# The last 156 words of a hand-written order, rearranged: an attention and dense layer on one core

## The chip, the cores and the metric

The kernel runs on one core of a Trainium2 chip. The metric is the device time of one execution in microseconds (us), the median of several runs. The core's engines have queues of their own and run each queue in order: TensorE (PE, with its weight loads shown as PEld), VectorE (DVE), ScalarE (ACT), GpSimd (POOL) and SyncE (SP), which here issues nearly all DMAs.

## The reference, cut to what matters

```python
xn = layernorm(x)                                   # x: [1, 2048, 512], bf16
# A: attention in 4 segments of 512 tokens, 32 heads of 16, with a memory M, z
q, k, v = xn @ wq, xn @ wk, xn @ wv
for s in range(4):
    p = softmax(qs @ ks.T * scale + causal_mask);  a_dot = p @ vs
    a_mem = (phi(qs) @ M) / (phi(qs) @ z + 1e-6)    # memory of the segments before
    o = g * a_mem + (1 - g) * a_dot                 # g = sigmoid(beta), by head
    M += phi(ks).T @ vs;  z += phi(ks).sum()
A = o @ wo
B = silu(xn @ w1) @ w2                              # dense layer, 1792 wide
return x + A + B
```

## The kernel before, in words

The 2048 tokens are four segments of four 128-token tiles. Channels lie in four groups `dt` of 128 (eight heads each), the dense layer's 1792 features in 14 tiles. Outputs of A and B are summed in one PSUM accumulation: an output tile of 128 tokens by 512 columns takes 18 products, 14 with the dense layer's `hT` and `w2`, 4 with the attention's `oT` and `wo`. They may come in any order.

Nothing is scheduled automatically. One long string, `ORDER` (lines 16 to 98), is a list of words, and a loop (line 795) emits the piece of work that each word names. The order of the words is therefore the order in every engine's queue. The words at the end of the list are:

- `S76` and so on: scores of a batch (line 653): PE's products, then ACT's exponential of 128x2048 and POOL's causal mask. All scores share one tile of four PSUM banks, `psS`.
- `E15`, `O15`: products of the weights with V for the even and odd heads (line 687). `Ev15`, `Oa15` copy the sums out (DVE, ACT), and SP moves rows of them by small DMAs (`zraw`, `oraw`).
- `h3.11.0`, `ha`, `hv`: the dense layer's first product (two halves), its tanh on ACT (line 457), its multiply on DVE (line 462).
- `R0.2`, `W0`, `R1.*`, `W1`: reciprocals and weights of the softmax sums (DVE, lines 525 and 531).
- `z3.1`, `d3.1`: SP spreads the weights over partitions by two DMAs each into an `spr` buffer (line 542; four buffers). `zv`, `dv` multiply with them (lines 554 and 564), `n3.1` is the memory's product on PE, `nv` adds it into `oT` (line 573).
- `o3.0.12`: product 12 of output tile 0 of segment 3, all 512 columns. `oc` is a half of the columns, `od` a quarter. `oh12.1` is product 12 of the last tile, right half; the last tile is made as two halves of 256 columns.
- `xl3.0`: SP loads 128 rows of x for the residual into `x_res` (line 579). `st3.0`: DVE evicts the output tile, adding the residual (line 586), and SP stores it (line 591). `sh0`, `sh1`: the same for the halves of the last tile (lines 633 and 637).

Output tiles 0 and 1 of the last segment lie in banks of a pool of four (`pp`), which the dense layer, the sums and the memory's products also use. Tile 2 and the two halves of tile 3 lie in a last allocation of the four-bank tile of the scores, called `fin`, one bank each:

```python
                if "fin" not in st:
                    st["fin"] = psatt.tile([P, 4, L], F32, name="psS")
                st["psO", *key] = st["fin"][:, half or j, 0:width]
```

The kernel takes away the wait of a product for the eviction of another output in `fin` (lines 617 to 621); the wait of an eviction for the products is left to the framework. A pool hands out its buffers in the order in which they came free in the list. After a word of scores the products are whole (128x128 weights, line 322); after `E` or `O` they are issued as four products of 32 weight columns each (line 324).

Of the kernel before, what the change touches and what calls it, by code (L numbers as in the profile page):

```python
# [91 lines left out]
S73 h3.2.1 ha3.2 Ev14 oc2.2.5.1 o2.1.2 o2.2.16 o2.1.6 hv3.12 h3.8.0 o2.2.10 st2.2 hv3.2 o2.1.1 o2.1.5 h3.8.1 ha3.8 hv3.8  # L92
S79 o2.1.0 O14 Ov14 od2.1.12.2 s3 sv3 r3.1 o2.1.7 r3.3 h3.7.0 r3.2 r3.0 oc2.1.10.0 od2.1.12.3 o2.1.3 w3
S77 h3.6.0 R0.0 oc2.1.11.0 h3.7.1 R0.1 ha3.7 h3.6.1 hv3.7 d3.2 o2.1.14 R0.3 h3.9.0 ha3.6 hv3.6 o2.1.15
S76 o2.1.8 d3.0 d3.1 h3.9.1 o2.1.9 oc2.1.10.1 h3.13.0 ha3.9 od2.1.12.0 oc2.1.11.1 h3.13.1 xl3.3 hv3.9 o3.0.12 od2.1.12.1 o2.1.4 o3.0.1 o2.1.13 ha3.13
S75 dv3.2 R0.2 W0 o3.0.7 hv3.13 o3.0.4 h3.10.0 z3.2 o2.1.16 h3.10.1 z3.1 o3.0.2 o3.0.8 dv3.0 o3.0.9 o3.0.0 z3.0 ha3.10 hv3.10
S78 o3.0.5 h3.11.0 o2.1.17 st2.1 h3.11.1 E15 o3.0.6 o3.2.1 oh1.1 o3.1.8 Ev15 ha3.11 oc3.0.3.1 oh0.1 O15 oh12.1 o3.2.3 o3.2.5 hv3.11 zv3.1 oh5.1 o3.2.8 n3.2 Oa15 oh13.0 o3.1.3 o3.1.12 dv3.1 zv3.2 nv3.2 o3.2.7 oc3.0.11.1 oc3.0.11.0 oh9.0 n3.0 oh16.0 n3.1 zv3.0 o3.2.9 o3.1.1 oc3.1.0.1 o3.1.13 o3.2.0 oc3.1.0.0 o3.2.12 o3.2.6 nv3.0 od3.1.11.2 nv3.1 oh11.1 o3.1.14 oh15.1 o3.2.11 oh0.0 R1.1 R1.0 oh10.0 o3.0.14 od3.0.10.2 oh8.0 od3.1.11.3 d3.3 oh15.0 od3.0.10.0 R1.3 o3.1.6 R1.2 oc3.1.9.0 oc3.1.9.1 o3.1.5 oh2.0 o3.1.10 W1 oh14.0 o3.2.13 oh1.0 o3.1.15 oh5.0 o3.0.15 o3.0.16 dv3.3 z3.3 od3.0.10.1 o3.2.15 xl3.1 o3.2.16 zv3.3 o3.2.2 n3.3 oh11.0 od3.1.11.1 oh3.1 oh10.1 oh6.0 oh4.1 nv3.3 o3.1.4 od3.0.10.3 oh4.0 oh12.0 o3.2.4 o3.0.13 oc3.0.3.0 oh3.0 o3.0.17 xl3.0 st3.0 o3.2.14 od3.1.11.0 oh7.0 o3.2.17 oh17.0 oh7.1 sh0 o3.2.10 o3.1.2 oh2.1 o3.1.7 o3.1.16 st3.2 o3.1.17 oh17.1 st3.1 oh6.1 oh13.1 oh14.1 oh16.1 oh8.1 oh9.1 sh1
"""


# [733 lines left out]
```

## Time and profile before

| | |
|---|---|
| median of 3 runs | 228.55 us (228.1 to 229.02) |
| the profiled execution | 229.09 us |
| its span, first to last instruction | 227.4 us |
| granted TensorE clock | 1.00 |
| PE busy | 217.2 us (96%) |
| DVE, ACT, POOL busy | 177.7, 198.0, 113.9 us |
| first product of S76, the first word on the changed lines | 200.01 us |
| last product begins | 223.32 us |
| last DVE eviction, `sh1` | 223.88 us, 0.41 long |
| last store issued | 224.77 us |

The span is what the profile shows; the run's time also has what lies around it, 1.7 us here. The page gives the busy time of each engine; the chain of waits follows the work that ended last back from the end; the timeline lists instructions in order of time. An instruction's line in it ends with the idle time before it and what ended that.

### The profile page before, as it was taken

What the parts mean: (1) busy time and instruction counts of PE and PEld (TensorE: products, weight loads), DVE (VectorE), ACT (ScalarE), POOL (GpSimd) and SP (SyncE); (2) the same over time, 40 slices, a digit from 0 to 9 for tenths busy, and PEclk for the clock granted to TensorE, in tenths of its full rate; (3) what the DMA queues carried; (4) which work ended last, traced back from release to release, by engine and by line L of the source; (5) the groups of instructions that cost most, each with busy time, mean ns of one, the idle gap of its engine ahead of it and who ended that gap; (6) DMA issues with size and microseconds to landing.
All of it is one profiled execution on the core that took longest, in us unless ns stands there. A gap on an engine that the chain in (4) does not pass through costs nothing.

```text
span 227.4 us, 7543 instructions
## 1 busy us (share of the span) xinstructions
PE 217.2 (96%) x3124; PEld 112.9 (50%) x3152; DVE 177.7 (78%) x351; ACT 198.0 (87%) x179; POOL 113.9 (50%) x173
## 2 busy tenths in 40 slices
PE   8999999999999999999999999999999999999993
PEld 8666645545534434444444434445444444445662
DVE  5799899987787897658798798747676888887834
ACT  3799998999999999999999899999999989897000
POOL 6059647667454673665644577546474265342000
PEclk9999999999999999999999999999999999999999
DMA  6992429323215213404314212141032212024122
GB/s 181 361 381 68 77 52 299 60 55 57 61 22 158 72 35 47 96 15 112 41 40 113 75 53 58 35 117 42 22 100 66 88 36 84 29 63 130 29 90 94
DMA packets 34787, 20.55 MB, mean 90 GB/s; under 512 B 15680, under 2 KB 34240, under 8 KB 34752
## 3 DMA queue, kind: packets, MB, share of 16 engines
q1 hardware_dynamic: 32128, 17.45, 28.3%
q10 hardware_dynamic: 2624, 2.62, 3.6%
q8 instruction: 24, 0.39, 0.8%
q14 instruction: 11, 0.09, 0.1%
HBM read 9.96 MB, written 2.10 MB: 53 GB/s over the span
## 4 chain that ended last, share of the span: by engine, by line
PE 62%; ACT 11%; DVE 11%; DMA 8%; issue 4%; SPq 2%; POOL 0%; DVEq 0%
PE ps L322 18%; PE psO L322 14%; PE psS L662 9%; ACT Pb L669 8%; PE ps L324 8%; PE psO L324 6%; PE psV L696 6%; DMA x_hi<-in_A_x_dram 4%; DMA spr<-rz 3%; ACT th L457 2%; DMA x_res<-in_A_x_dram 2%; DVE stats L272 1%; DVE o_out L586 1%; DVE kT L361 1%; PE psM L324 1%
## 5 line engine op out<-in xcount | busy, mean ns | idle before, releaser
L669 ACT ACTIVATE Pb<-psS 128x2048 bf16<-128x2048 f32 x80 | 150.2, 1878 | 5.8 <-PE psS L662 5.1
L677 POOL TENSOR_SCALAR_AFFINE_SELECT Pb<-Pb 128x512 bf16<-128x512 bf16 (+1 forms) x112 | 80.1, 729 | 85.1 <-ACT Pb L669 83.7
L462 DVE SCALAR_TENSOR_TENSOR hT<-th,ps 128x512 bf16<-128x512 bf16 x56 | 37.8, 679 | 14.1 <-ACT th L457 13.7
L322 PE MATMUL ps<-xnT,w_sb 128*128 128x512 bf16 (+1 forms) x177 | 43.3, 340 | 0.8 <-issue 0.5
L322 PE MATMUL psO<-w_sb,hT 128*128 128x512 bf16 (+2 forms) x139 | 36.1, 340 | 0.7 <-issue 0.5
L457 ACT ACTIVATE th<-ps 128x512 bf16<-128x512 f32 x56 | 32.8, 597 | 0.5 <-PE ps L322 0.4
L324 PE MATMUL psO<-w_sb,hT 128*32 128x128 bf16 (+2 forms) x468 | 26.7, 300 | 0.0
L322 PEld LDWEIGHTS <-w_sb 128*128 128x128 bf16 x184 | 17.1, 98 | 16.3 <-issue 3.3
L696 PE MATMUL psV<-Pb,Vz 128*32 128x128 bf16 (+3 forms) x512 | 23.1, 300 | 0.4 <-DVE oT L573 0.2
L322 PEld LDWEIGHTS <-hT 128*128 128x128 bf16 x149 | 13.6, 97 | 16.9 <-issue 4.8
L324 PE MATMUL ps<-xnT,w_sb 128*32 128x512 bf16 (+1 forms) x384 | 21.8, 329 | 0.0
L324 PEld LDWEIGHTS <-hT 128*32 128x32 bf16 x636 | 15.7, 97 | 9.7 <-issue 1.7
L696 PEld LDWEIGHTS <-Vz 128*32 128x32 bf16 x512 | 13.0, 96 | 10.6 <-issue 1.4
L662 PE MATMUL psS<-qT,kT 16*128 16x128 bf16 (+3 forms) x256 | 17.3, 301 | 0.9 <-ACT Pb L669 0.8
L662 PE MATMUL psS<-qT,kTo 32*128 32x384 bf16 (+3 forms) x256 | 17.2, 299 | 0.6 <-ACT Pb L669 0.2
L362 POOL TENSOR_SCALAR kTo<-kT,pm_odd 128x512 bf16<-128x512 bf16 x16 | 11.9, 747 | 8.2 <-DVE kT L361 7.3
L322 PE MATMUL ps<-xnT,wk_sb 128*128 128x512 bf16 (+1 forms) x66 | 15.4, 328 | 0.7 <-issue 0.5
L322 PE MATMUL ps<-wv_sb,xnT 128*128 128x512 bf16 x48 | 14.3, 380 | 0.6 <-issue 0.2
L662 PEld LDWEIGHTS <-kT 16*128 16x128 bf16 x256 | 5.9, 91 | 16.7 <-issue 16.2
L361 DVE CAST kT<-ps 128x512 bf16<-128x512 f32 x15 | 10.2, 687 | 4.6 <-PE ps L322 4.3
L586 DVE SCALAR_TENSOR_TENSOR o_out<-psO,x_res 128x512 bf16<-128x512 f32 x14 | 9.6, 687 | 5.3 <-PE psO L322 2.8
L719 DVE CAST oraw<-psV 128x512 bf16<-128x512 f32 x16 | 11.0, 688 | 3.4 <-PE psV L696 3.3
(105 smaller groups left out, 298.3 us busy)
## 6 DMA issues: line engine op xcount, KB each, us to landing
spr<-rz SPq DMA_DIRECT2D x56, 64.0 KB
x_res<-in_A_x_dram SPq DMA_DIRECT2D x16, 128.0 KB
out_dram<-o_out SPq DMA_DIRECT2D x15, 128.0 KB
w_sb<-in_B_w_dram SPq DMA_DIRECT2D x1, 1792.0 KB
w_sb<-in_B_w_dram ACTq DMA_DIRECT2D x1, 1792.0 KB
x_hi<-in_A_x_dram SPq DMA_DIRECT2D x2, 512.0 KB
oraw<-odd SPq DMA_DIRECT2D x64, 16.0 KB
wv_sb<-in_A_wv_dram SPq DMA_DIRECT2D x2, 256.0 KB
```

The costliest lines, as they stand in the source:

```text
L322: return [nc.tensor.matmul(out, lhsT=lhsT, rhs=rhs, start=start, stop=stop, skip_group_check=True)]
L324: nc.tensor.matmul(out[c : c + 32], lhsT=lhsT[:, c : c + 32], rhs=rhs, start=start, stop=stop, tile_position=(0, c), skip_group_check=True,)
L361: copy(out=kT[:, dt, :], in_=sts[s].pop(("k", dt))[:, :])
L362: nc.gpsimd.tensor_scalar(out=kTo[:, dt, :], in0=kT[:, dt, :], scalar1=pm_odd[:, 0:1], scalar2=1.0, op0=ALU.mult, op1=ALU.mult,)
L457: nc.scalar.activation(out=th[:], in_=sts[s]["h", ft][:, :], func=AF.Tanh, scale=0.5)
L462: nc.vector.scalar_tensor_tensor(out=st["hT"][:, ft, :], in0=st.pop(("th", ft))[:], scalar=1.0, in1=st.pop(("h", ft))[:, :], op0=ALU.add, ...
L586: out = nc.vector.scalar_tensor_tensor(out=o_out[:], in0=st.pop(("psO", j)), scalar=0.5, in1=st["x", j][:], op0=ALU.mult, op1=ALU.add)
L662: nc.tensor.matmul(psS[:, g, c0 : c0 + nq], lhsT=kk[rows, dt, kt * P : (kt + 1) * P], rhs=st["qT"][rows, dt, kt * P : L], start=True, stop ...
L669: exp = nc.scalar.activation(out=Pb[:, :, :], in_=psS[:, :, :], func=AF.Exp, scale=SCALE)
L677: mask = nc.gpsimd.affine_select(out=blocks, in_=blocks, compare_op=ALU.is_ge, fill=0.0, base=0, pattern=[[0, blocks.shape[1]], [1, P]], c ...
L696: nc.tensor.matmul(psV[32 * g : 32 * g + 32, kt * P : L], lhsT=Vzs[s % 2][:, kt, 4 * dt + g, par : par + 2, :].rearrange("p a d -> p (a d) ...
L719: copy(out=oraw[:], in_=sts[s].pop(("psV", 0))[:, :])
```

## The change

Four lines of `ORDER` are replaced by three with the same 171 words. The first 15 words keep their places. In the new order the scores S78 and the dense products `h3.11` come earlier, the eviction `st2.1` of segment 2's last open tile comes much later, the `z` moves go 0, 1, 2 in place of 2, 1, 0, `dv3.2` comes after `dv3.0`, and the five stores come in the order `sh1`, `sh0`, `st3.0`, `st3.2`, `st3.1` with up to four words of products between them; in the old order `st3.0`, `sh0`, `st3.2`, `st3.1`, `sh1`, with up to seven.

```diff
-S76 o2.1.8 d3.0 d3.1 h3.9.1 o2.1.9 oc2.1.10.1 h3.13.0 ha3.9 od2.1.12.0 oc2.1.11.1 h3.13.1 xl3.3 hv3.9 o3.0.12 od2.1.12.1 o2.1.4 o3.0.1 o2.1.13 ha3.13
-S75 dv3.2 R0.2 W0 o3.0.7 hv3.13 o3.0.4 h3.10.0 z3.2 o2.1.16 h3.10.1 z3.1 o3.0.2 o3.0.8 dv3.0 o3.0.9 o3.0.0 z3.0 ha3.10 hv3.10
-S78 o3.0.5 h3.11.0 o2.1.17 st2.1 h3.11.1 E15 o3.0.6 o3.2.1 oh1.1 o3.1.8 Ev15 ha3.11 oc3.0.3.1 oh0.1 O15 oh12.1 o3.2.3 o3.2.5 hv3.11 zv3.1 oh5.1 o3.2.8 n3.2 Oa15 oh13.0 o3.1.3 o3.1.12 dv3.1 zv3.2 nv3.2 o3.2.7 oc3.0.11.1 oc3.0.11.0 oh9.0 n3.0 oh16.0 n3.1 zv3.0 o3.2.9 o3.1.1 oc3.1.0.1 o3.1.13 o3.2.0 oc3.1.0.0 o3.2.12 o3.2.6 nv3.0 od3.1.11.2 nv3.1 oh11.1 o3.1.14 oh15.1 o3.2.11 oh0.0 R1.1 R1.0 oh10.0 o3.0.14 od3.0.10.2 oh8.0 od3.1.11.3 d3.3 oh15.0 od3.0.10.0 R1.3 o3.1.6 R1.2 oc3.1.9.0 oc3.1.9.1 o3.1.5 oh2.0 o3.1.10 W1 oh14.0 o3.2.13 oh1.0 o3.1.15 oh5.0 o3.0.15 o3.0.16 dv3.3 z3.3 od3.0.10.1 o3.2.15 xl3.1 o3.2.16 zv3.3 o3.2.2 n3.3 oh11.0 od3.1.11.1 oh3.1 oh10.1 oh6.0 oh4.1 nv3.3 o3.1.4 od3.0.10.3 oh4.0 oh12.0 o3.2.4 o3.0.13 oc3.0.3.0 oh3.0 o3.0.17 xl3.0 st3.0 o3.2.14 od3.1.11.0 oh7.0 o3.2.17 oh17.0 oh7.1 sh0 o3.2.10 o3.1.2 oh2.1 o3.1.7 o3.1.16 st3.2 o3.1.17 oh17.1 st3.1 oh6.1 oh13.1 oh14.1 oh16.1 oh8.1 oh9.1 sh1
+S76 o2.1.8 d3.0 d3.1 h3.9.1 o2.1.9 oc2.1.10.1 h3.13.0 ha3.9 od2.1.12.0 oc2.1.11.1 h3.13.1 xl3.3 hv3.9 o3.0.12 ha3.13 o3.0.8 R0.2 o2.1.17 o3.0.6 o3.0.2 o2.1.4
+S75 o3.0.9 h3.11.0 hv3.13 h3.10.0 o2.1.16 h3.10.1 o2.1.13 o3.0.0 oc3.0.3.0 ha3.10
+S78 od2.1.12.1 W0 h3.11.1 z3.0 dv3.0 o3.0.1 hv3.10 E15 o3.0.4 ha3.11 od3.0.10.1 dv3.2 oc3.0.3.1 z3.1 z3.2 Ev15 o3.0.13 o3.0.5 oh4.0 o3.2.12 oh0.0 oh2.1 hv3.11 zv3.0 oh5.1 od3.0.10.0 O15 dv3.1 oh3.1 oh7.1 n3.0 zv3.1 oh6.1 o3.2.13 Oa15 oh6.0 oh12.0 od3.0.10.3 o3.1.13 d3.3 o3.1.1 nv3.0 o3.1.8 oh3.0 n3.2 od3.0.10.2 o3.2.10 oh0.1 o3.1.3 zv3.2 o3.2.8 oh8.0 nv3.2 R1.1 oh13.1 oh10.1 od3.1.11.1 o3.0.7 oh16.0 R1.2 oh16.1 oh14.0 oc3.1.9.1 R1.3 R1.0 oh14.1 oh13.0 oh2.0 o3.1.16 o3.1.12 oh9.0 o3.2.0 o3.1.10 o3.2.7 oh1.1 n3.1 oh5.0 o3.1.2 oh10.0 o3.1.6 o3.1.4 W1 o3.2.9 oh12.1 nv3.1 oc3.1.0.1 z3.3 xl3.1 oh7.0 od3.1.11.0 o3.0.14 o3.2.14 oh8.1 oc3.0.11.0 st2.1 dv3.3 zv3.3 o3.0.16 o3.2.4 o3.2.11 o3.2.2 oh11.0 oh15.0 oh9.1 n3.3 oh15.1 xl3.0 o3.1.5 oh11.1 oh4.1 nv3.3 o3.2.15 oh1.0 o3.0.15 oh17.1 od3.1.11.2 o3.2.16 oh17.0 oc3.0.11.1 o3.2.1 o3.2.3 o3.0.17 o3.2.5 o3.2.17 sh1 o3.2.6 o3.1.15 oc3.1.9.0 od3.1.11.3 sh0 o3.1.7 st3.0 o3.1.17 o3.1.14 st3.2 oc3.1.0.0 st3.1
```

## The prediction

> **What bounds the kernel now.** I read, in this order, the page's busy times, the busy time by stretch over the last 27 us, the chain that ended last, and the timeline of the end. The first 15 words of the changed list are the old ones, so nothing before 202.5 us of the span (start of `o3.0.8`) can move.
>
> ```profile
> PE 217.2 (96%) x3124; PEld 112.9 (50%) x3152; DVE 177.7 (78%) x351; ACT 198.0 (87%) x179; POOL 113.9 (50%) x173
> ```
>
> ```profile
> 205.00:210.00 5.00, 5.00 (x98) 2.56 (x100) 3.58 (x7) 3.54 (x4) 1.27 (x2) 1.00 0.39 120
> 210.00:215.00 5.00, 5.00 (x128) 3.12 (x120) 4.21 (x10) 0.59 (x1) 0.00 (x0) 1.00 0.16 43
> 215.00:220.00 5.00, 5.00 (x148) 3.45 (x144) 2.52 (x7) 0.00 (x0) 0.00 (x0) 1.00 0.37 111
> 220.00:223.60 3.60, 3.60 (x96) 2.30 (x88) 2.08 (x5) 0.00 (x0) 0.00 (x0) 1.00 0.09 28
> 223.60:227.40 3.80, 0.00 (x1) 0.00 (x0) 0.69 (x2) 0.00 (x0) 0.00 (x0) 1.00 0.36 116
> ```
>
> Columns: the stretch, its length, busy us of PE, PEld, DVE, ACT, POOL, then the granted clock. PE is full to 223.60 at clock 1.00. Laying its products end to end from S76 (200.01), at 0.216 us for 512 columns (0.43 for two: 216.27, 216.38 and 216.59 in the timeline), I find no wait for data, only about 0.2 us at each change between score tiles and the rest. So 223.60 is a floor that the same products in another order can't undercut. What is left is the 3.78 us behind it.
>
> ```profile
> 208.37 3.75 DMA spr<-rz
> ...
> 212.21 0.44 DVE oT L554
> ...
> 216.91 0.60 SPq L542
> 217.51 0.04 issue
> 217.56 0.46 SPq L579
> 218.01 0.04 issue
> 218.06 3.60 DMA x_res<-in_A_x_dram
> ```
>
> ```profile
> 221.75 0.69 DVE L586 SCALAR_TENSOR_TENSOR o_out<-psO,x_res 128x512 bf16<-128x512 f32 x1 [1.52 <-PE psS L324]
> ...
> 222.35 0.41 DVE L633 SCALAR_TENSOR_TENSOR o_half<-psS,x_res 128x256 bf16<-128x256 f32 x1
> ...
> 222.69 0.68 DVE L586 SCALAR_TENSOR_TENSOR o_out<-psS,x_res 128x512 bf16<-128x512 f32 x1
> ...
> 223.21 0.39 PE L324 MATMUL psS<-w_sb,hT 128*32 128x256 bf16 x8
> 223.28 0.68 DVE L586 SCALAR_TENSOR_TENSOR o_out<-psO,x_res 128x512 bf16<-128x512 f32 x1
> 223.41 0.92 SPq L591 DMA_DIRECT2D out_dram<-o_out  x2
> 223.88 0.41 DVE L633 SCALAR_TENSOR_TENSOR o_half<-psS,x_res 128x256 bf16<-128x256 f32 x1
> 224.77 0.34 SPq L637 DMA_DIRECT2D out_dram<-o_half  x1
> ```
>
> The five evictions stand on DVE without a gap: 0.60 us from a full one to the next, 0.34 after a half. The first waited for its x_res, whose load took 3.60 us; but the last, `sh1`, could not have begun before PE's end plus 0.05 (the row of `st2.1`: product done 207.55, eviction 207.60), that is 223.65, and began 223.88. So the late load costs 0.23 at the end, not the 1.5 us that the chain suggests. From the last issue at 224.77 the store lands at 226.53 by the landing records (1.76; full stores took 1.73 to 1.80), and the closing of the program takes 0.85 to 227.38.
>
> **The change, part by part.**
>
> *Products.* Same words, so the same 479 products from S76 on. Whole and 32-column forms both take 0.216 us for 512 columns, so the seven words that change form with S78's earlier place cost 0, and the changes of form stay as many. No term.
>
> *The scores move.* Between `o3.0.12` and S75 there are now five full products (1.08 us) for three and a quarter (0.70): S75 comes 0.38 later, at 203.74. From S75 to S78 there is 2.27 of products for 2.38: S78 comes at 206.45 for 206.18. ACT was idle before both exponentials (0.46 and 0.44 us, waiting for PE), so they shift with the scores, S78's to 206.89 to 208.77, and POOL's mask to 208.90 to 209.54. Queued behind: `oh4.0`, first user of the four banks that this exponential reads, arrives at 208.84 with the banks ready at 208.82; `O15` arrives at 206.45 + 0.33 + 2.75 = 209.54, and started 0.05 after the mask before (209.27, 209.32). It can start at 209.59: **+0.05 us**. If that cover goes, each further tenth of lateness is a tenth. Bounds 0 to 0.15.
>
> *DVE.* `R0.2` comes before `hv3.13`, `dv3.2` only after `hv3.10`. Walking DVE with its row durations: `hv3.13` ends 204.64 and `h3.10.0`, which takes its bank, arrives at 204.73; `hv3.10` ends 207.28, `E15` arrives at 207.48; `nv3.0` ends 211.6, `n3.2` arrives at 211.9. All hidden by PE's own work, with 0.04 to 0.3 us to spare.
>
> *SP's queue.* It loses `st2.1` ahead of the moves of `zraw` (0.45 us), which goes between the two last x_res loads instead; the three `z` moves are reordered. `z3.0` takes the free buffer, `z3.1` that of `dv3.0` (free at 205.25), `z3.2` that of `dv3.2` (free at 207.62), so `z3.2` is issued at 207.68 and 208.33 in place of `z3.0`'s 207.73 and 208.37: SP loses nothing. That slot is the one whose landing took 3.75 us; half-moves otherwise land about 2.1 after issue. If the slot is late again, `z3.2` lands at 212.1, `nv3.2` ends at 213.37, and `oh16.0`, which reads it, arrives at 213.55: hidden by 0.13. Behind it `R1.*` waits for `zraw` (213.1), `W1` ends by 215.5 (before: 216.24), and `d3.3` then `z3.3` go out at 214.7 to 216.75 (before to 216.91). `z3.3` lands at 218.8; `n3.3` arrives on PE at 219.13 and ends 219.51, `nv3.3` 219.55 to 220.25, and `oh17.1`, first reader of the last quarter of oT, arrives at 220.43. Hidden by 0.13. I put **0** for these, bounds 0 and 0.3.
>
> *The x_res loads.* `xl3.0` leaves at 218.4 (before 218.06) behind `st2.1`'s store; with the 3.60 us of the old one it is there at 222.0, and `st3.0` needs it at 223.0. So the 0.23 above comes back, but the next part takes it.
>
> *The end.* In the list the five stores stand apart, but the four banks of the last outputs are one tile, and an eviction waits for the last product written to any of them: in the old program `sh0` waits for `oh7.1`, a product of another bank. So `sh1`, complete at `oh17.1` (220.7), waits for `o3.2.17`, the word before it (222.27), and starts at 222.32. Then the queue alone sets the pace: `sh0` 222.66, `st3.0` 223.00, `st3.2` 223.60, `st3.1` 224.20 to 224.88, though its last product ends at 223.65. Before, `sh1` ended at 224.29. The new last store would be issued at 224.91, for 224.77: before, SP stood idle 0.37 us before its fifth store with nothing that the profile shows; if it does so again, 225.08. It is a full store: 1.73 to 1.80. Landing 226.66 to 226.88, for 226.53: **+0.13 to +0.35**, the 0.05 of `O15` being in these times, and I take +0.2: nearer the lower end, since the idle 0.37 shows once only.
>
> Sum: span 227.4 + 0.2 = 227.6. The profiled execution took 229.09 (1.7 around its span), 0.54 over the median shown; I put +0.2 on the median: 228.75.
>
> The Trainium skill, "PSUM — Partial Sum Buffer", section "Summary: rules for kernel authors", says that to read PSUM while matmuls run one should target a different bank and guard by bank. By that rule the evictions would wait only for their own banks, which is the first rival; no row of this trace shows the chip reading one bank of this tile while another is written.
>
> **Rivals.**
>
> 1. *The stores do spread.* Were each eviction released by its own last product: `sh1` 220.75, `sh0` 221.13, `st3.0` 222.0, `st3.2` 222.55, `st3.1` 223.70 to 224.39, issued 224.42, landed 226.18, span 227.03: -0.36, 228.2. For it: the positions of the words. Against it: the wait of `sh0` in the old program.
> 2. *Slower: the late slot decides.* A landing one packet late, as with the 3.75 and the 3.60, hits a half of `z3.3`. PE is in order, so all behind `oh17.1` waits. It decides from about 0.3 us late: a landing 1.2 late (220.0) gives `zv3.3` and `nv3.3` until 221.28, PE stands 0.9, and with my 0.2 the time is 229.65. For it: both late rows lie on this queue within 10 us. Against: in the old trace the `z3.3` slot came in time.
> 3. *Thin covers in the middle.* Several of the margins of 0.04 to 0.13 are overrun, PE loses 0.3 to 0.6: about 229.2. For it: margins below the scatter of the landings. Against: PE lost nothing at equally thin places before (`O15` began 0.05 behind its mask).
> 4. *The new order does nothing for the end.* `x_res` late again by more than a microsecond beyond 3.60, `st3.0` after 223: each tenth is a tenth at the end; about 229.0 for 0.25.
>
> **How the numbers follow.** Forecast 0.50 (228.4 to 229.0 around 228.75), rival 1 0.14, rival 2 0.16, rival 3 0.13, rival 4 0.04, and 0.03 for a gain that I can't place. About 0.5% is what a measurement can tell from no change: faster means under 227.4, slower over 229.7. The gain is capped near 0.4 us by PE's floor, so faster gets 0.03. Slower gets three fourths of rival 2 (the landings that are later than 1.2, or hit with rival 3's margins used up) and a third of rival 3: 0.17 with rounding up. The rest, 0.80, is within. Range 228.1 (rival 1) to 229.8 (just over rival 2's worked case).
>
> **What would show it.** Right: the last product ends at 223.6 to 223.7; `O15` begins within 0.1 of 209.6; five evictions without a gap from about 222.3, `st3.1` last at 224.2, an issue about 224.9. Rival 1: `sh1` near 220.8 and gaps on DVE. Rival 2 or 3: idle PE before products that read oT, with DVE or a DMA as releaser, and a last product past 223.9. Wrong altogether: a change before 202 us, a lower clock, or SP blocked at `z3.2`.

## The result and the profile after

| | before | after |
|---|---|---|
| median of 22 runs each | 228.50 us (227.87 to 230.96) | 229.31 us (228.46 to 231.63) |
| ratio after to before | | 1.0044, 95% interval 1.0025 to 1.0063 |
| the profiled execution, its span | 229.09, 227.4 us | 230.19, 228.5 us |
| first product of S76 | 200.01 us | 200.22 us |
| end of the last product | 223.60 us | 224.37 us |
| from there to the end of the span | 3.78 us | 4.11 us |

The changed order is slower: the medians differ by 0.8 us (0.35%), and the ratio estimated from all the runs is 0.44% over 1, with an interval that leaves out 1. A caution on reading: the start of S76, ahead of which the two orders are the same, lay anywhere from 198.76 to 200.83 us in the 14 profiles of this study (where that comes from is shown at e7). So spans of single profiles are not compared below, only what lies behind S76: 27.37 us before (227.38 less 200.01), 28.26 after.

The busy times of the page of after, and its row for the queue that fetches instructions:

```profile
PE 220.9 (97%) x3149; PEld 113.7 (50%) x3149; DVE 177.1 (77%) x351; ACT 198.0 (87%) x179; POOL 113.8 (50%) x173
...
q8 instruction: 24, 0.39, 0.7%
```

PE's 220.9 us can't be set against the 217.2 of before: the page of before lacks some of PE's products (3124, for 3152 weight loads).

The busy time by stretch of after, with the same columns as before:

```profile
205.00:210.00 5.00, 5.00 (x93) 2.74 (x95) 2.61 (x6) 4.18 (x4) 1.27 (x2) 1.00 0.40 113
210.00:215.00 5.00, 4.67 (x136) 3.42 (x132) 3.67 (x9) 0.58 (x1) 0.00 (x0) 1.00 0.09 22
215.00:220.00 5.00, 5.00 (x128) 3.22 (x124) 3.43 (x8) 0.00 (x0) 0.00 (x0) 1.00 0.41 119
220.00:224.37 4.37, 4.37 (x108) 2.48 (x96) 2.00 (x5) 0.00 (x0) 0.00 (x0) 1.00 0.10 28
224.37:228.50 4.13, 0.00 (x0) 0.00 (x0) 1.24 (x3) 0.00 (x0) 0.00 (x0) 1.00 0.40 129
```

PE is full and at clock 1.00 everywhere but in one stretch, 210 to 215, where 0.33 us is missing. Before, that stretch was full. The timeline of after shows the place (start, length, engine, line, operation; last, the idle time before it and what ended that):

```profile
212.99 0.43 DVE L554 TENSOR_TENSOR oT<-spr,oraw 128x512 bf16<-128x512 bf16 x1 [1.20 <-issue]
...
213.52 0.69 DVE L573 TENSOR_TENSOR oT<-ps,oT 128x512 bf16<-128x512 f32 x1
...
214.27 0.51 PE L324 MATMUL psS<-wo_sb,oT 128*32 128x256 bf16 x12 [0.33 <-DVE oT L573]
```

This is `zv3.2`, `nv3.2` and then `oh16.0`, the first product that reads the third quarter of `oT`. By the pace of the products ahead of it `oh16.0` was due at 213.75 and began at 214.27: 0.51 us lost. (The view says 0.33, since it lets the product before run on until its modelled end.) DVE had idled 1.20 us with nothing shown but "issue"; the chain of waits of after says what it waited for (start, length, what):

```profile
208.65 3.14 DMA spr<-rz
211.79 1.20 issue
219.06 0.97 PE psS L324 x24
223.82 1.19 DVE o_out L586 x2
```

The second half of `z3.2` went out at 208.65. In the landing records (the updates of the semaphore that tells of a DMA's landing) eight of its nine updates had come 2.07 us later, and the ninth came 4.26 us later, at 212.91: one piece was late; `zv3.2` began 0.08 behind it. The end, in the timeline of after:

```profile
223.06 0.76 DVE L633 SCALAR_TENSOR_TENSOR o_half<-psS,x_res 128x256 bf16<-128x256 f32 x2 [2.07 <-PE psS L324]
...
223.51 0.82 SPq L637 DMA_DIRECT2D out_dram<-o_half  x2
...
223.73 0.68 DVE L586 SCALAR_TENSOR_TENSOR o_out<-psO,x_res 128x512 bf16<-128x512 f32 x1
...
224.33 0.68 DVE L586 SCALAR_TENSOR_TENSOR o_out<-psS,x_res 128x512 bf16<-128x512 f32 x1
224.44 1.61 SPq L591 DMA_DIRECT2D out_dram<-o_out  x3
224.93 0.68 DVE L586 SCALAR_TENSOR_TENSOR o_out<-psO,x_res 128x512 bf16<-128x512 f32 x1
```

All five evictions begin only behind 223.01, where `o3.2.17` ends, and then follow each other without a gap, as before. The stores that the list sets apart, with products between them, leave within 2.2 us of each other. The last issue is at 225.68 and lands at 227.63.

So of the 0.88 us that this profile has more behind S76 than the one of before, 0.04 is at `O15`, 0.51 at `oh16.0`, and 0.33 lies behind the last product.

### The profile page after: what moved, and what is told of

It reads as the page before. It is cut to its first block, busy times and chain, and to the rows that moved or that the text cites. A ratio compares the mean times of both kernels' runs of the same rounds, so it can differ in the third digit from the quotient of the medians.

```text
span 228.5 us, 7564 instructions
## 1 busy us (share of the span) xinstructions
PE 220.9 (97%) x3149; PEld 113.7 (50%) x3149; DVE 177.1 (77%) x351; ACT 198.0 (87%) x179; POOL 113.8 (50%) x173
## 4 chain that ended last, share of the span: by engine, by line
PE 62%; ACT 12%; DVE 11%; DMA 6%; issue 4%; SPq 3%; POOL 0%; DVEq 0%; ACTq 0%
PE ps L322 16%; PE psO L322 13%; ACT Pb L669 9%; PE psS L662 8%; PE ps L324 8%; PE psO L324 7%; PE psV L696 6%; DMA x_hi<-in_A_x_dram 4%; DMA spr<-rz 3%; ACT th L457 3%; PE psS L324 2%; SPq L542 1%; DVE stats L272 1%; DVE hT L462 1%; DVE kT L361 1%
## 5 line engine op out<-in xcount | busy, mean ns | idle before, releaser
L322 PE MATMUL ps<-xnT,w_sb 128*128 128x512 bf16 (+1 forms) x186 | 45.4, 342 | 0.0
L322 PE MATMUL psO<-w_sb,hT 128*128 128x512 bf16 (+2 forms) x147 | 38.8, 343 | 0.0
L324 PE MATMUL psO<-w_sb,hT 128*32 128x128 bf16 (+2 forms) x476 | 27.6, 301 | 0.0
L324 PE MATMUL ps<-xnT,w_sb 128*32 128x512 bf16 (+1 forms) x376 | 21.2, 328 | 0.0
L324 PEld LDWEIGHTS <-hT 128*32 128x32 bf16 x644 | 16.2, 97 | 9.4 <-issue 1.7
L322 PE MATMUL ps<-xnT,wk_sb 128*128 128x512 bf16 (+1 forms) x69 | 16.1, 330 | 0.0
L322 PE MATMUL ps<-wv_sb,xnT 128*128 128x512 bf16 x53 | 15.6, 380 | 0.0
L726 DVE CAST odd<-psV 128x512 bf16<-128x512 f32 x15 | 10.3, 687 | 3.5 <-PE psV L696 3.4
```

The lines of the kernel that those rows point to most:

```text
L322: return [nc.tensor.matmul(out, lhsT=lhsT, rhs=rhs, start=start, stop=stop, skip_group_check=True)]
L324: nc.tensor.matmul(out[c : c + 32], lhsT=lhsT[:, c : c + 32], rhs=rhs, start=start, stop=stop, tile_position=(0, c), skip_group_check=True,)
L726: copy(out=odd[:], in_=sts[s].pop(("psV", 1))[:, :])
```

## The experiments

Two questions were open: whether the stall at `oh16.0` is a property of the order or of one execution, and whether the wait on all four banks of `fin` is what keeps the stores from spreading. The table has what the profile of each kernel shows behind S76, in us. "Stall" is the time a product began after its turn; `O15` has 0.04 in every kernel with the changed order, and is left out. e7 and e8 were run twice.

| kernel | stall | last product to end | S76 to end | ratio to before, 95% interval |
|---|---|---|---|---|
| before; once more | none; none | 3.78; 3.85 | 27.37; 27.44 | |
| after; once more | `oh16.0` 0.51; 0.25 | 4.11; 4.05 | 28.26; 27.92 | 1.0044 (1.0025 to 1.0063) |
| e1_later | `oh17.1` 0.47 | 4.11 | 28.20 | 1.0044 (1.0015 to 1.0073) |
| e2_own_bank | none | 3.31 | 26.94 | 1.0014 (0.9986 to 1.0041) |
| e3_both | `oh17.1` 0.27 | 3.71 | 27.61 | 1.0020 (1.0000 to 1.0041) |
| e4_fetch | none | 4.04 | 27.69 | 1.0024 (1.0004 to 1.0045) |
| e5_slack | none | 3.92 | 27.55 | 1.0014 (0.9995 to 1.0034) |
| e6_act_loads | `o3.0.17` 0.48 | 3.73 | 27.81 | 1.0048 (1.0023 to 1.0073) |
| e7_swap; e7_again | none; none | 3.63; 3.62 | 27.26; 27.25 | 1.0029 (1.0005 to 1.0054); 1.0029 (1.0003 to 1.0054) |
| e8_before_own; e8_again | none; none | 3.43; 3.73 | 27.02; 27.32 | 0.9987 (0.9964 to 1.0009); 1.0014 (0.9993 to 1.0034) |

**Both kernels once more.** No edit; one execution each.

> The changed kernel once more, for its scatter. Theory (PE's wait for the late piece hangs on where the 16 KB transfer falls, from run to run): from S76 to the end 27.7 to 28.4 us; PE idle between 0 and 0.5 us, at oh16.0 or oh17.1, the four-bank evictions without a gap, 4.0 to 4.2 us from the last product's end to the end. Rival (a fixed cost of the order): PE idle 0.51 at oh16.0 again.

> The kernel before once more. Theory: no idle PE behind S76 over 0.1 us and 27.1 to 27.5 us from S76 to the end, though one landing or more is late by over a microsecond, at another place. Rival (before waits as often, and its first profile was a lucky one): PE idle 0.2 to 0.5 at a reader of oT.

They took 230.09 and 229.24 us, and the stalls and ends are within what the theories named. In after the second half of `z3.2` is late again (3.99 us, its other pieces 2.09) and `oh16.0` stalls 0.25. In before the move in the same slot, `z3.0`, is late too (3.53), and no product stalls for it: it is the order that puts a product with little cover behind this slot.

**e1_later: the readers of the third quarter later.**

```diff
-... o3.0.7 oh16.0 R1.2 oh16.1 oh14.0 ... oh2.0 o3.1.16 o3.1.12 ... oh1.1 n3.1 ...
+... o3.0.7 R1.2 oh14.0 ... oh2.0 o3.1.12 ... oh1.1 oh16.0 oh16.1 o3.1.16 n3.1 ...
```

> Edit: oh16.0, oh16.1 and o3.1.16, the three first readers of oT's third quarter, stand behind oh1.1, about 1.5 us of products later; all else as in the changed kernel. Theory (the loss is PE standing 0.51 us at oh16.0 for the late half of z3.2): the half is still late (zv3.2 near 213), PE has no idle time there, the last product ends near 223.85 in place of 224.37, and the ratio to before falls from 1.0044 to about 1.002. Rival (the wait only moves on to oh17.1, the first reader of the last quarter): PE idle at oh17.1 by 0.3 or more, ratio 1.003 to 1.0045. Rival (the loss is all in the stores at the end): ratio unchanged at 1.004.

There is no stall at `oh16.0`, but another of the same size came, and the ratio is the one of after. The first rival's numbers fit, but it is not the old lateness that moved on. In this profile the second half of `z3.2` landed in 2.07 us, so that the wider cover at `oh16.0` was not needed (in e7_swap below it is). The timeline of e1_later:

```profile
212.66 3.13 SPq L730 DMA_DIRECT2D oraw<-odd  x4
215.83 0.68 SPq L542 DMA_DIRECT2D spr<-rz  x1
```

```profile
220.14 0.42 DVE L554 TENSOR_TENSOR oT<-spr,oraw 128x512 bf16<-128x512 bf16 x1 [0.95 <-DMA spr<-rz]
220.67 0.69 DVE L573 TENSOR_TENSOR oT<-ps,oT 128x512 bf16<-128x512 f32 x1
```

```profile
221.42 0.29 PE L324 MATMUL psS<-wo_sb,oT 128*32 128x256 bf16 x4 [0.28 <-DVE oT L573]
```

SP's four `oraw` issues took 3.13 us here, 2.45 before: one of them alone took 1.27 in place of 0.59. So `d3.3` and `z3.3` behind them went out 0.68 late, `z3.3` landed on time by its own measure (2.06) but at 220.02, and `oh17.1`, with a cover foretold as 0.13, stood for it. A second thin cover stood behind the first.

What delays a move's piece at one time and SP's issue at another? In the records a transfer of 16 KB on the instruction queue (q8, 24 on the page) comes about once for every 256 of PE's instructions (products and weight loads) and takes 0.9 to 1.6 us. In after one starts at 209.95, 1.30 us behind the issue of `z3.2`; in e1_later one starts at 214.48, just ahead of the slow issue (214.52 to 215.79). Over the 14 profiles the last half-move of this slot was late in six of the seven where the transfer began 1.1 to 1.3 us behind its issue (3.45 to 4.26 us in place of 2.1), and in one of the seven where it began 1.7 us or more behind it. The rest of the records makes the tie firmer. At a half-move some 75 us earlier, where the order is the same in all kernels, the transfer began 0.6 to 1.1 us behind the issue in eight profiles, and the half was late in all eight (3.28 to 4.08 us); it began 1.8 to 2.0 us behind in six, and the half was late in none. And over the whole of the 14 traces from 30 us on, 925 of SP's DMAs (those that transpose left out) had such a transfer in flight beside them, and in 215 of them the last piece came 0.6 us or more behind the one before it; of the other 2080 it did so in 29. Of their 85 issues that took over 0.3 us more than usual, 82 overlapped a transfer. So the transfer makes lateness likely, not certain. The Trainium skill, "Runtime: NRT & Kernel Launch", section "Instruction fetch mechanics", says that instructions are fetched in blocks of 256 (16 KiB) by a queue of the sequencer's own while the current block runs, at a cost that is mostly hidden. The traces agree with the size and the count, and behind S76 no product of PE is seen to wait for them (the stalls of the table all wait for a late move). What these runs show besides is that other DMAs pay.

**e4_fetch: the transfers at another time.** The whole products between S76, S75 and S78 are issued as four of 32 columns; the work is the same, PE has 168 instructions more (84 products and 84 weight loads; the expectation's 162 was a little low).

```diff
-        narrow[0] = now == "cols"
+        narrow[0] = now == "cols" or (now == "whole" and i > words.index("S76"))
```

> Edit: the products between S76 and S75 and between S75 and S78 are issued as four of 32 weight columns instead of whole, which takes the same PE time but 162 more PE instructions; the order is the changed kernel's. Theory (a spread half is late because a 16 KB transfer of the instruction queue, one per about 256 PE instructions, runs while it is in flight): that transfer starts near 206.4 in place of 209.95, z3.2 lands by 211, PE does not stand at oh16.0; the transfer after it starts near 211.9 in place of 215.3 and makes another move late (zraw, then z3.3), with PE idle at oh17.1 possibly. Rival (the lateness belongs to z3.2's place on SP's queue, or to chance): z3.2's second half lands near 212.9 as before and PE stands 0.5 at oh16.0.

The page of e4_fetch has one transfer more:

```profile
q8 instruction: 25, 0.41, 0.7%
```

Behind S76, which began 1.12 us earlier here than in after, they now start at 204.87, 209.95, 214.18 and 219.48; the theory had the first two near 205.3 and 210.8 by this profile's clock. The one at 209.95 comes 2.42 us behind the issue of `z3.2`'s second half, which lands in 2.07 us, and `oh16.0` does not stall. Others are late in its place: an `x_res` load issued at 203.6 (3.58 us, its other pieces 2.02) and an `oraw` move issued at 213.09 (3.07 and 1.85). Nothing with thin cover hangs on those. So the stall at `oh16.0` goes when the transfer moves, without any change to the order. It is one profile, and not proof by itself: in e2 below `z3.2` is on time as well (transfer 1.73 us behind its issue), without this edit. The counts above say how far to trust it. S76 to the end is 0.23 to 0.57 less than in the two profiles of after; the ratio, 1.0024, can't be told from that of after.

**e2_own_bank: each eviction waits for its own bank alone.** The order is the changed one. The framework is told that an eviction of one output in `fin` doesn't depend on the products of another.

```diff
         if s == LAST and j >= 2:
+            fin_mm.extend((key, mm) for mm in mms)
...
             fin_out.append(((j,), out))
+            alone((j,), out)
...
+    def alone(key, out):
+        for other, mm in fin_mm:
+            if other != key:
+                tc.declare_no_dep(out.ins, mm.ins, reason="the outputs lie in banks of their own")
```

> Edit: an eviction of an output in the four banks of fin no longer waits for products of another output, in another bank; all else as in the changed kernel. Theory (evictions are held by the tile's last product, so five follow each other without a gap): sh1 starts near 221.5 in place of 223.06, there are gaps on DVE, st3.1 starts 0.05 after the last product (224.42) in place of 224.93, the last issue comes 0.4 to 0.5 earlier, ratio about 1.002. Rival (the end is set by the landings of the stores, not by their issue): st3.1 starts early and the time stays, ratio 1.004.

The timeline of e2_own_bank, where the last product ends at 222.39:

```profile
219.52 0.81 DVE L641 SCALAR_TENSOR_TENSOR o_half<-psS,x_res 128x256 bf16<-128x256 f32 x2 [0.50 <-PE psS L324]
220.69 0.69 DVE L586 SCALAR_TENSOR_TENSOR o_out<-psO,x_res 128x512 bf16<-128x512 f32 x1 [0.37 <-PE psO L324]
221.30 0.69 DVE L586 SCALAR_TENSOR_TENSOR o_out<-psS,x_res 128x512 bf16<-128x512 f32 x1
222.44 0.69 DVE L586 SCALAR_TENSOR_TENSOR o_out<-psO,x_res 128x512 bf16<-128x512 f32 x1 [0.45 <-PE psO L324]
```

Now the stores do stand apart: the first eviction begins 2.87 us before the last product ends (in after: 1.31), three of the four rows are released by PE, and the last begins 0.05 us behind the last product. The end falls from 4.11 to 3.31. So the wait on all four banks is what kept the stores together. DVE reads one bank of the tile while PE writes another, at no loss: an eviction takes 0.69 us as before, and S76 to PE's end is 23.63 for 23.59, `O15`'s 0.04 among it. The Trainium skill, "PSUM — Partial Sum Buffer", section "Summary: rules for kernel authors", which asks for a guard by bank, is borne out by this trace. In the times the gain shows only as a tendency, 1.0014 for 1.0044 with intervals that overlap. The middle is untouched, and in this profile `z3.2` happened to be on time (2.07); that it was late in other runs is likely, but not shown.

**e3_both and e5_slack: the two together, and wider covers.** e3 has both edits. e5 moves, on top, `oh17.1`, `oh17.0`, `o3.0.17` and `o3.2.17` about 1 us later, each with its eviction right behind it.

```diff
-... o3.0.15 oh17.1 od3.1.11.2 o3.2.16 oh17.0 oc3.0.11.1 o3.2.1 o3.2.3 o3.0.17 o3.2.5 o3.2.17 sh1 o3.2.6 ... sh0 o3.1.7 st3.0 o3.1.17 ...
+... o3.0.15 od3.1.11.2 o3.2.16 oc3.0.11.1 o3.2.1 o3.2.3 o3.2.5 oh17.1 sh1 oh17.0 sh0 o3.0.17 st3.0 o3.2.17 o3.2.6 ... o3.1.7 o3.1.17 ...
```

> Edit: both of the former. Theory: the two parts add up, last product near 223.85, st3.1 at 223.9, ratio 0.999 to 1.000, equal to before or a little faster. Rival (they share one cause): ratio 1.002.

> Edit: the former one with both, and besides the first readers of oT's last quarter (oh17.1, oh17.0, o3.0.17, o3.2.17) stand 1.0 us of products later, each eviction right behind its last product. Theory (what is left is PE waiting at oh17.1 for a late z3.3, 0.27 in the run with both): PE has no idle time over 0.1 us behind S76, from S76's first product to the last product's end 23.6 to 23.7 us, from there to the end 3.3 to 3.5, so 26.9 to 27.2 from S76 to the end against 27.37 before and 28.26 in the changed kernel; ratio 0.998 to 0.9995. Rival (the landings of the stores grow with their spread): 27.5 or more, ratio 1.001 to 1.002.

e3 still stalls 0.27 at `oh17.1`, from the same cause as e1 (an `oraw` issue of 1.07 us with a transfer at 214.56), and its ratio, 1.0020, is the rival's and not the theory's. With the cover of e5 nothing stalls, though an `oraw` issue took 1.40 us there too. But its end is 3.92, over the 3.3 to 3.5 of the theory, for a reason of its own. The timeline of e5_slack:

```profile
221.39 0.76 DVE L641 SCALAR_TENSOR_TENSOR o_half<-psS,x_res 128x256 bf16<-128x256 f32 x2 [0.82 <-PE psS L324]
222.53 0.69 DVE L586 SCALAR_TENSOR_TENSOR o_out<-psO,x_res 128x512 bf16<-128x512 f32 x1 [0.39 <-DMA x_res<-in_A_x_dram]
```

`st3.0` waits for its row of x, `xl3.0`, which stands behind the store of `st2.1` in SP's queue and lands at 222.44. The issue of that store took 1.58 us in place of 0.38, with a transfer beside it from 218.29 on. Two full evictions queue behind it, so the last begins 0.50 us after the last product. This is the prediction's rival 4, in a kernel where the four banks no longer hide it. The 27.55 us and the ratio 1.0014 are those of e5's rival, but not for its reason: the five stores landed in 1.55 to 1.87 us, no longer than in after.

**e7_swap and e7_again: e5 with the last two rows of x exchanged.**

```diff
-... z3.3 xl3.1 oh7.0 ... oh15.1 xl3.0 o3.1.5 ...
+... z3.3 xl3.0 oh7.0 ... oh15.1 xl3.1 o3.1.5 ...
```

> The version with the wider covers and the waits by bank (e5_slack), with only the loads of the last two rows of x exchanged in SP's order: xl3.0 goes out right behind z3.3 and xl3.1 behind the store of st2.1. Theory (the order itself costs nothing; its late landings and the wait on all four banks do): st3.0 no longer waits for a row that lands at 222.44 in that profile, the five evictions close up, st3.1 starts within 0.1 us of the last product, the end of the products to the end of the span is 3.3 to 3.5 us in place of 3.92, and from the first product of S76 to the end of the span it is 27.0 to 27.2 us (before: 27.37 and 27.44). Ratio 0.997 to 1.000. Rival (spread stores cost more than their waits, for example because each of the stores competes with the others): the tail stays at 3.8 or more although the evictions are early, and the ratio is 1.001 or more.

> e7_swap once more: it has no stall behind S76 but 0.04 us and 27.26 us from S76 to the end of the span, 0.1 to 0.2 us less than the kernel before, and yet a median 0.8 us above it. If late landings come and go from run to run in the changed order even with the wider covers, the ratio is again 1.001 to 1.004 and this profile shows a stall of 0.2 us or more at a product of row 16 or 17. If the first ratio was scatter, it is 0.998 to 1.001, and the profile shows no such stall.

The timeline of e7_again, whose last product ends at 222.90:

```profile
221.05 0.76 DVE L641 SCALAR_TENSOR_TENSOR o_half<-psS,x_res 128x256 bf16<-128x256 f32 x2 [1.08 <-PE psS L324]
...
222.95 0.69 DVE L586 SCALAR_TENSOR_TENSOR o_out<-psO,x_res 128x512 bf16<-128x512 f32 x1
```

`st3.0` no longer waits, the last eviction begins 0.05 us behind the last product, and S76 to the end is 27.25 in both profiles, 0.1 to 0.2 less than before. The end of 3.62 is still over the 3.3 to 3.5 expected: the last two stores took 2.0 to 2.1 us to land; e2's last took 1.69.

In e7_swap the second half of `z3.2` is as late as in any profile (4.34), and `oh16.0`, which stands later by e1's edit, doesn't stall: `nv3.2` ends at 214.88, `oh16.0` begins at 215.96. An `oraw` issue took 1.37 and 1.15 us in the two, and `oh17.1` doesn't stall either. So the covers of e1 and e5 do what they are for.

The times contradict the profiles: 1.0029 twice, 0.8 and 0.9 us above before. Neither expectation holds: the ratio is the rival's, the profile the theory's. The 22 runs fall into two groups, 9 up to 228.7 and 13 from 229.1 up; of the 44 runs of before beside them 11 were at 229.1 or above. Each profile is of one group: e7_swap (229.78 us) began S76 at 200.80, e7_again (228.23 us) at 199.26, and the two are alike behind it. Of these 1.54 us, 0.35 came in the first 23 us and 1.20 in one stretch between 136 and 154 us, by the same mechanism as at `oh16.0`. The chain of waits of e7_swap:

```profile
131.61 4.08 DMA spr<-rz
...
135.78 0.84 DVE oT L554
136.62 0.61 DVE oT L573
...
137.27 0.73 PE psV L705 x16
```

The half-move took 4.08 us, and 2.06 in e7_again. This is the earlier half-move that was counted above, and it explains much of the scatter of S76's start: where it landed in 2.1 us (six profiles) that stretch takes 16.97 us, where in 3.28 to 3.38 (four) 17.58, where in 3.53 to 4.08 (four) 18.17. The rest is the first 23 us, which differ by up to 1.06, and one stall of 1.0 at 99 us in e1. Both profiles of before had 0.6 us of it, those of after 0.6 and 1.2. The order there is that of before in every kernel, so why it should come more often with e7's list is not settled by these runs; that other executions, which left no trace, stall behind S76 is not excluded either.

**e8_before_own and e8_again: the old order, with the waits by bank.** The same edit as e2, on the kernel before.

> The kernel before, in its own order, with only the eviction's wait on products of other banks taken away. If the wait on all four banks costs the same whatever the order, the end of the products to the end of the span falls from 3.78 and 3.85 to 3.4 to 3.6 us (st3.1 no longer queues ahead of sh1, which then starts within 0.1 us of its last product in place of 0.28 us), and the ratio is 0.997 to 0.999. If the kernel before keeps its evictions off that wait by its order already, the tail stays at 3.75 to 3.85 and the ratio at 0.999 to 1.001; then the wait by tile is a cost of the changed order alone.

> e8_before_own once more, to tell a gain of 0.13% from none. If its end of 3.43 us in place of 3.78 and 3.85 is what the times show, the ratio is again 0.997 to 1.000, the products' end to the end of the span is 3.35 to 3.55 us, and no product stalls behind S76. If the first ratio was scatter of the part ahead of S76, it is 1.000 or more although the end is as short.

The timeline of e8_before_own, whose last product ends at 223.40:

```profile
221.05 0.69 DVE L586 SCALAR_TENSOR_TENSOR o_out<-psO,x_res 128x512 bf16<-128x512 f32 x1 [1.27 <-DMA x_res<-in_A_x_dram]
...
222.69 0.69 DVE L586 SCALAR_TENSOR_TENSOR o_out<-psO,x_res 128x512 bf16<-128x512 f32 x1
223.45 0.42 DVE L641 SCALAR_TENSOR_TENSOR o_half<-psS,x_res 128x256 bf16<-128x256 f32 x1
```

`sh1` begins 0.05 behind its last product, and the end is 3.43. In e8_again the row of x for `st3.0` lands 0.41 us later by the last product (2.04 before its end for 2.45), the evictions close up behind it again, `sh1` begins 0.19 late, and the end is 3.73, over the 3.35 to 3.55 expected. The times say 0.9987 and 1.0014: no change that can be told. No version of this study beats the kernel before; and with the waits by bank the old order's end was in one of two profiles nearly as short as the spread one's, 3.43 for 3.31.

**e6_act_loads: a miss.** The kernel before, with the last two loads of x issued from ACT's queue, which is idle then, right behind `Oa15`.

```diff
-        nc.sync.dma_start(out=sts[s]["x", j][:], in_=x_flat[t * P : (t + 1) * P, :])
+        eng = nc.scalar if s == LAST and j < 2 else nc.sync
+        eng.dma_start(out=sts[s]["x", j][:], in_=x_flat[t * P : (t + 1) * P, :])
```

> Edit, on the kernel before: the two last x_res loads are issued from ScalarE's queue behind Oa15 instead of from SP behind z3.3; all else as before. Theory (the late load costs only the 0.23 us by which sh1 missed PE's end): st3.0 starts near 220.9, sh1 0.05 after the last product, ratio 0.998 to 0.9995. Rival (the chain of waits is right, the load's 1.5 us of idle DVE are on the path): ratio 0.994. Rival (SP's idle time before its fifth store and the landing set the end): ratio 1.000.

It is slower, 1.0048. The timeline of e6_act_loads:

```profile
211.63 1.06 SPq L712 DMA_DIRECT2D zraw<-odd  x2
213.19 2.45 SPq L731 DMA_DIRECT2D oraw<-odd  x4
```

```profile
221.75 0.40 PE L324 MATMUL psO<-wo_sb,oT 128*32 128x512 bf16 x4 [0.30 <-DVE oT L573]
```

SP stands idle from 212.69 to 213.19, and goes on 0.01 behind the late piece of `z3.0` (issued 209.19, landed 213.18). In the program a DMA is made to wait for the one that used its semaphore eight DMAs before; two loads put in between shift that rotation, so that the first `oraw` move now waits for the very move that is late. `z3.3` follows late, and `o3.0.17` stalls 0.48. The part that the theory was about came true: `sh1` begins 0.06 behind the last product. Moving a DMA off a busy queue turned a harmless late landing into a wait of the whole queue.

## Why the prediction was right, and where its sum was off

The forecast was 228.75 and no difference of more than 0.5%; it is 229.31 and 0.44%, inside the range of 228.1 to 229.8 but at the upper part of it. The difference itself was put at +0.2 us and measured at +0.8, so the answer holds by little (the interval, 0.25% to 0.63%, reaches past 0.5%), and the time lies in the range because the range took in the rivals, not because of the sum. By its steps:

1. *Products as a floor.* Right: the same products (in 476 instructions for 479, one word less being issued as four), no wait but the two named below, PE at clock 1.00. S76 to PE's end is 24.14 for 23.59, and 0.55 of stalls is all of the difference.
2. *The later scores, `O15` +0.05.* Right: 0.04 in nine profiles with the changed order.
3. *DVE's thin covers, 0.* Right in that no product waited for `hv3.13`, `hv3.10` or `nv3.0` in any profile.
4. *SP's slot with the late landing: "hidden by 0.13", put at 0, bounds 0 and 0.3.* This is the term that was mis-sized. The mechanism was followed to the instruction: late slot, `z3.2`, `nv3.2`, `oh16.0`. But two sizes in it were off. The single landing of 3.75 us was taken for the price of the slot; it landed in 4.26 and 3.99 in the two profiles of after. And "SP loses nothing" was wrong: the half was to go out 8.32 us behind the start of S76 (208.33) and went out 8.43 behind it in both, with 0.18 us between `z3.0` and `z3.1`, where SP's queue has two waits. That left 0.02 of the cover. Landing and issue together come to 0.49 and 0.22 over the cover; the stalls were 0.51 and 0.25, the first over the upper bound. A cover of 0.13 against a landing that takes 2.1 us when on time and 3.45 to 4.34 when late in this slot is no cover, and a 0 there had to be a share of that scatter. By this, what happened is rival 3's case (thin covers overrun by 0.3 to 0.6, 229.2), put at 0.13. The same goes for the 0.13 in front of `oh17.1`, which held in both profiles of after and was overrun in e1 and e3; rival 2's late landing of `z3.3` itself did not show, a late issue did.
5. *The loads of x.* Right: `st3.0` waited for nothing but the evictions ahead.
6. *The end, +0.13 to +0.35.* The mechanism was right in all parts: `sh1` waits for `o3.2.17` (223.01, 223.06), five evictions without a gap, SP idle again before the fourth store. The last issue stands 1.32 us behind PE's end, for 1.26 to 1.43 foretold. Only the last landing is over, 1.95 for 1.73 to 1.80. The 1.76 of before's last store was misread: it is a half, the other half took 1.59, and its last piece came 0.22 behind the others. The last full store of after has the same (1.74 without that piece). In 13 of the 14 profiles the last store has such a piece, 0.12 to 0.50 late, and each time a short transfer on another instruction queue (q14 on the page, 0.3 to 0.6 us) begins while it is in flight; in e2 that transfer began before the last store, which took 1.69, and the store ahead of it was late by 0.25. So the end is +0.33 and, in the second profile, +0.20 to +0.27 by which profile of before is taken; +0.2 was taken.

Rival 1 (the stores spread) was turned down for the right reason: take the wait on all four banks away and it comes true, with an end of 3.31 (e2). But the sentence beside it, that no row shows one bank of this tile being read while another is written, is contradicted by the rows that the prediction shows: `st3.2` is evicted from `psS` from 222.69 to 223.37, and PE writes `psS` from 223.21, in the bank of `sh1`. The chip did it before the change; it is the wait alone that held the evictions.

That the sum of the terms, 0.05 + 0.25 to 0.51 + 0.20 to 0.33, comes near the measured 0.8 speaks for them. It isn't proof that they are all: e7 has none of them but `O15` in its profiles and is still 0.29% slower in the times. Stalls ahead of S76, in the part that all kernels share, scatter the times by as much as these terms; whether they came more often in the runs of one kernel than of another is not known, and that remainder stays open.

## What to carry to other kernels

A cover is worth what it exceeds the scatter of the thing that it covers, not what one profile leaves over: where a product's operand comes by a DMA that was late once, ask how late that slot may be, and leave room for it: in these profiles a late half-move cost up to 0.5 us behind S76 and up to 1.2 us ahead of it, and covers wider by about 1.5 us (`oh16.0`) and 1 us (`oh17.1`) were enough in the one and the three profiles that needed them. Before rearranging work so that outputs finish one by one, look at what an eviction waits for; where banks of one tile are guarded as one, the order alone gains nothing. And when a new order takes away one stall, look at once for the next thin cover behind it, for another late DMA can hit it.

## What the runs showed of the hardware

That PE's own instruction stream disturbs other engines' DMAs was not foreseen. About every 256 PE instructions 16 KB are fetched in 0.9 to 1.6 us; a DMA in flight then in about one case of four (215 of 925) has one last piece that comes 0.6 to 2.2 us behind its others (in the two places above a late half-move took 3.3 to 4.3 us, any other 2.1), or SP's issue is held. The timeline of e2_own_bank has one of the longest such issues, a load that otherwise takes 0.46 us, with a transfer at 217.33:

```profile
217.12 1.75 SPq L579 DMA_DIRECT2D x_res<-in_A_x_dram  x1
```

Behind S76 the transfers' time from the start of S76 differs by up to 0.6 us between two executions of one kernel, and so which DMA is hit can differ too; that fits the wider scatter of after, whose readers have less cover (the middle half of its 22 runs spans 1.5 us, of before's 0.8). It was shown for the profiles; for the runs without a trace it is an inference.
